# Load order, a copy in two halves, and a new instruction order in a four-layer transformer kernel

## The chip, the cores and the metric

The kernel runs on one core of a Trainium2 chip. A core has five engines that run side by side, each with its own in-order list of instructions: TensorE (PE, matrix products into PSUM), VectorE (DVE), ScalarE (ACT), GpSimd (POOL) and SyncE (SP, which here only issues DMA transfers). They wait for each other through semaphores. PSUM has eight banks of 512 columns. The metric is the time of one execution on the device in microseconds, as the median of several runs; smaller is better.

## What is computed

Two layers of linear attention (A) and two of a dense network with ReLU (B) alternate over a residual stream of 2048 tokens and 512 features:

```python
def _layernorm(x, axis=-1, eps=1e-5):
    m = jnp.mean(x, axis=axis, keepdims=True)
    v = jnp.var(x, axis=axis, keepdims=True)
    return (x - m) / jnp.sqrt(v + eps)
...
def _A_ref(x, wqkv, wo):          # 32 heads of 16
    ...
    phi = lambda t: jnp.where(t > 0, t + 1, jnp.exp(t)) + 1e-6
    pq, pk = phi(q), phi(k)
    kv = jnp.einsum("bhsd,bhse->bhde", pk, v)
    z = jnp.einsum("bhsd->bhd", pk)
    num = jnp.einsum("bhqd,bhde->bhqe", pq, kv)
    den = jnp.einsum("bhqd,bhd->bhq", pq, z)[..., None] + 1e-6
    o = num / den
    return (lambda x, *d: x.transpose(*d))(o, 0, 2, 1, 3).reshape(B, S, D) @ wo
def _B_ref(x, w1, w2):            # 1376 hidden features
    h = jnp.einsum("bsd,df->bsf", x, w1)
    h = jnp.maximum(h, zero)
    return jnp.einsum("bsf,fd->bsd", h, w2)
...
x = x + _A_ref(_layernorm(x, axis=-1), A_wqkv, A_wo)
x = x + _B_ref(_layernorm(x, axis=-1), B_w1, B_w2)
x = x + _A_ref(_layernorm(x, axis=-1), A_wqkv, A_wo)
x = x + _B_ref(_layernorm(x, axis=-1), B_w1, B_w2)
```

## The kernel before

**Tiles and chunks.** The 2048 tokens are 16 tiles of 128 (tile *i*), in four chunks of four. Tiles 0, 1, 2 and 3 are chunk 0; tiles 4 to 7 are chunk 1. Layers are numbered 0 to 3, and a step's full name has the layer ahead of it (`0.kproj2`).

**Loads.** All inputs stay in SBUF once loaded. `ld_x(lo, hi)` brings token tiles lo to hi-1 in one DMA, `ld_w` a slice of the attention weights. In this text they go by their keys: x0, x1 (one tile each), x2 (tiles 2 and 3), x4 (tiles 4 to 7), x8 and x12 (four tiles each); wka and wkb, the first and second half (by rows) of the K weights; wqa and wqb, the same of the Q weights; wv0, the V weights; wvl, one row of them broadcast to all partitions; wo, w1, w2a and w2b. wka is issued from ACT's queue, all other loads from SP's. SP issues in its own list's order, and each issue occupies it for about half a microsecond.

**The start of layer 0**, for each tile *i* (`ln_first`, L1668): `bnst` and `bnag` on DVE give mean and variance (L847, L848); `lnv` and `rstd` on ACT (or `veps` on DVE and `rstd` on POOL) the reciprocal root; `fnorm` on DVE the normed tile `xn` (L885). Tiles 0 to 5 are then transposed on PE: `trp` makes four 128x128 transposes into one PSUM bank, and `trev` copies the bank to `Tb`, on ACT for tiles 0 to 3 (`transpose_pe`, L905). Tiles 6 and 7 and all later ones are transposed by DMA, two tiles at a time: `tr1_1` is that of tiles 6 and 7, `tr2_0` and `tr2_1` those of chunk 2 (L898). `fill0` is eight products of zeros that keep PE running between `trp0` and `trp1` (L838).

Then come the projections. `kproj`*i* multiplies a tile by the K weights (four products of 512 columns, accumulated in a bank); for tiles 0 and 1 it is split by the weights' halves, `kproj0_0` (wka) and `kproj0_1` (wkb), so that the first can run before wkb is there (L973). The Q projection of chunk 0 runs in sixteen pieces `qh0_`*h_j_k*: tiles *2h* and *2h+1*, output block *j*, weight half *k* (wqa or wqb; L1196). Every K or Q bank is read by ACT twice, `_lin` (plus one) and `_exp`, and the larger is taken on DVE (`_em`, `_phi`), which gives phi. `wvless0` to `wvless3` on DVE subtract wvl from the V weights (L1110).

**Between layers 0 and 1.** `g` products sum phi(k) against the normed tiles; `gev` copies them out (L1141); `kv` and `kvmask` make the block-diagonal products, `m` multiplies them by wo, and `mev` copies the result `Mf` (L1166). `den` products give the denominators, `lnd` and `rdc` on ACT their reciprocals, and sixteen DMAs `spread`*t_j* broadcast these across partitions (L1223). `pqs` on DVE scales phi(q) (L1230), `fin`*i*`_0` and `fin`*i*`_2` are the halves of the output product of tile *i*, `resid` on DVE adds it to the stream, `sq` on ACT gives the squares for the next norm. From layer 1 on, products of 2x2 blocks are formed with seven multiplications instead of eight, and the sums that this needs are spread over ACT and DVE (names with `hv`, `hc`, `hs`, `p1` to `p7`, `c11` to `c22`).

**What sets the order.** The source creates operations in a fixed sequence, and each gets an index. A table `HINTS` (L63 on, about 1900 entries) adds a number to each, and each engine executes its operations strictly in order of the sum:

```python
op.prio = op.idx + HINTS.get(op.key, 0)      # L422
WINDOW = {PE: 1, ACT: 1, DVE: 1, POOL: 1, SP: 1}
```

An entry with "!" chooses the engine where there are two (0 or 1, an index into the operation's alternatives; for `trev`, `gev` and `mev` 0 is ACT and 1 is DVE). A planner (`_list_schedule`, L464) goes through these lists with assumed durations, hands out the PSUM banks, and so finds which waits have to be written. `LOAD_LATE` (L53) holds its assumptions on how late each load lands. Neither the assumed times nor the assumed lateness reach the chip; order, engines, banks and waits do.

Of the kernel before, what the change touches and what calls it, by code (L numbers as in the profile page):

```python
# [52 lines left out]
LOAD_LATE = {"x1": 320.0, "x2": 490.0, "wka": 780.0, "wkb": 540.0, "wqa": 1000.0, "x4": 1300.0, "wqb": 1260.0, "x12": 1060.0, "x8": 960.0, "wv0": 350.0}  # L53
# [9 lines left out]
HINTS = {"0.aqsum1": -43, "0.aqsum1!": 0, "0.aqsum2": -24, "0.aqsum2!": 0, "0.aqsum3": -126, "0.aqsum3!": 0, "0.aqsum4": 36,  # L63
# [302 lines left out]


class _Op:
# [1606 lines left out]
```

## Time and profile before

| | |
|---|---|
| runs | 262.16 us median of 3 (262.15 to 262.83) |
| the profiled execution, its own time | 262.21 us |
| its span, first to last instruction | 260.5 us |
| granted clock of TensorE | 1.000 of full speed |
| ACT, DVE, POOL: share of the span | 80%, 89%, 23% |
| DMA queue q1 (SP's): share of 16 engines' span | 35.8% |

In the views, PE is the matrix product, PEld the load of its weights, SPq the issue of a DMA. A row of the timeline reads: start and duration in us, engine, source line, operation, tile written <- tiles read, shape, how many are merged; in brackets, where there is one, the engine's idle time ahead of it and what ended it. A row of the chain in order of time reads: start, duration, what. A row of the DMA view ends with KB and us from issue to landing. A row of the windows reads: the stretch and its length, then the busy time of PE, PEld, DVE, ACT, POOL with the number of instructions, the granted clock, the DMA share and GB/s. A row of the waits reads: who <- for whom, us in total, times, longest. Most products have one source line (L953), so they are told apart by tiles and order.

### The profile page before, as it was taken

The page shows a single profiled execution, that of the slowest core. Times are in us where ns is not written, and L with a number is a line of the kernel's source. Part 1 is how long each engine was busy: PE and PEld are TensorE (multiplying, and loading weights), DVE is VectorE, ACT ScalarE, POOL GpSimd, SP SyncE. Part 2 cuts the span into 40 slices and gives each one's busy share as a digit, 9 for nine tenths or more (in the row PEclk, how much of TensorE's full clock was granted, in tenths as well). Part 3 has the DMA queues.
Part 4 walks back from the last instruction along what each step waited for, and adds up shares of the span by engine and source line. Part 5 has one row for each costly group of instructions (what it writes and reads, how often), then busy time and mean ns, then how long its engine had stood idle before and what let it go on. Part 6 is the DMA issues. An engine that isn't in the chain of part 4 may idle for free.

```text
span 260.5 us, 5888 instructions
## 1 busy us (share of the span) xinstructions
PE 255.3 (98%) x2176; PEld 198.9 (76%) x2176; DVE 230.7 (89%) x574; ACT 207.5 (80%) x446; POOL 60.0 (23%) x160
## 2 busy tenths in 40 slices
PE   7999999999999999999999999999999999999995
PEld 3555577834778898889888878774488988988884
DVE  4999998799989999999999899759999997876874
ACT  4999999579989988998899799786999946882200
POOL 4110000028745007240330340002875000000000
PEclk9999999999999999999999999999999999999999
DMA  7767951744351430434031030057442514200104
GB/s 206 277 148 140 330 189 21 183 101 97 68 67 32 87 58 12 91 42 63 0 60 25 0 73 11 3 113 172 95 80 50 82 23 128 56 20 3 81 3 161
DMA packets 45980, 22.46 MB, mean 86 GB/s; under 512 B 35872, under 2 KB 44416, under 8 KB 45952
## 3 DMA queue, kind: packets, MB, share of 16 engines
q1 hardware_dynamic: 45680, 21.83, 35.8%
q8 instruction: 17, 0.28, 0.4%
q10 hardware_dynamic: 272, 0.26, 0.4%
q14 instruction: 11, 0.09, 0.1%
HBM read 7.14 MB, written 2.10 MB: 35 GB/s over the span
## 4 chain that ended last, share of the span: by engine, by line
PE 85%; ACT 5%; DVE 4%; DMA 4%; SPq 1%; issue 1%
PE ps L953 84%; DVE xres L960 2%; DMA Tb<-xn 2%; SPq L1227 1%; ACT sqscr L968 1%; DMA big<-rdc 1%; DMA xin<-in_A_x_dram 1%; ACT xn L895 1%; DVE bst L847 1%; PE ps L914 0%; ACT rdc L1217 0%; DVE big L1235 0%; ACT escr L935 0%; ACT ps L700 0%; ACT lnd L1215 0%
## 5 line engine op out<-in xcount | busy, mean ns | idle before, releaser
L953 PE MATMUL ps<-w,big 128*128 128x256 bf16 (+1 forms) x256 | 32.3, 273 | 0.0
L968 ACT ACTIVATE sqscr<-xres 128x512 bf16<-128x512 f32 x48 | 29.8, 622 | 3.2 <-DVE xres L1623 1.6
L953 PE MATMUL ps<-big,xn 128*128 128x256 bf16 (+1 forms) x224 | 32.1, 288 | 0.0
L700 ACT ACTIVATE ps<-ps 128x512 f32<-128x512 f32 (+1 forms) x41 | 23.1, 573 | 10.5 <-PE ps L953 10.2
L953 PE MATMUL ps<-Mf,big 128*128 128x512 bf16 x128 | 28.6, 380 | 0.0
L953 PEld LDWEIGHTS ps<-w,big 128*128 128x128 bf16 (+1 forms) x256 | 25.0, 98 | 3.1
L953 PEld LDWEIGHTS ps<-big,xn 128*128 128x128 f16 x224 | 21.4, 98 | 6.3 <-issue 1.1
L953 PE MATMUL ps<-Tb,w 128*128 128x256 f16 x160 | 24.3, 273 | 0.0
L1436 DVE TENSOR_TENSOR big<-ps,escr 128x512 bf16<-128x512 f32 (+1 forms) x38 | 22.7, 601 | 1.3 <-ACT escr L1455 0.6
L953 PEld LDWEIGHTS ps<-Mf,big 128*128 128x128 bf16 x128 | 12.2, 98 | 14.5 <-ACT Mf L1166 0.5
L953 PE MATMUL ps<-xn,w 128*128 128x256 f16 x160 | 23.0, 273 | 0.0
L953 PE MATMUL ps<-xn,xin 128*128 128x256 f16 x160 | 22.7, 273 | 0.0
L953 PE MATMUL ps<-wqkv,Tb 128*128 128x512 bf16 (+1 forms) x96 | 20.3, 344 | 0.2 <-ACT Tb L920 0.2
L895 ACT ACTIVATE xn<-xres,nbias,rstd 128x512 f16<-128x512 f32 x24 | 19.1, 813 | 1.4 <-POOL nbias L879 1.4
L1455 ACT ACTIVATE escr<-ps 128x512 f32<-128x512 f32 (+1 forms) x38 | 18.7, 535 | 1.8 <-PE ps L953 1.8
L877 POOL TENSOR_TENSOR rstd<-veps,nhalf 128x2 f32<-128x2 f32 x24 | 18.2, 759 | 7.0 <-DVE veps L875 5.5
L869 POOL TENSOR_SCALAR mean<-s 128x2 f32<-128x2 f32 x24 | 7.2, 301 | 54.4 <-DVE xres L960 52.8
L1424 ACT ACTIVATE big<-ps 128x512 bf16<-128x512 f32 (+1 forms) x38 | 18.9, 527 | 0.4 <-PE ps L953 0.3
L953 PE MATMUL ps<-w,Tb 128*128 128x96 bf16 (+2 forms) x176 | 17.3, 225 | 0.6 <-DMA Tb<-xn 0.6
L953 PEld LDWEIGHTS ps<-Tb,w 128*128 128x128 bf16 x160 | 15.5, 98 | 2.3 <-DVE w L1384 0.2
L1445 ACT ACTIVATE big<-big 128x1024 bf16<-128x1024 bf16 (+1 forms) x16 | 14.3, 904 | 3.5 <-DVE big L1436 3.3
L953 PEld LDWEIGHTS ps<-xn,w 128*128 128x128 bf16 x160 | 15.5, 98 | 1.9 <-DVE xn L1402 0.2
(146 smaller groups left out, 639.6 us busy)
## 6 DMA issues: line engine op xcount, KB each, us to landing
big<-rdc SPq DMA_DIRECT2D x32, 128.0 KB, 2.7
xin<-in_A_x_dram SPq DMA_DIRECT2D x3, 512.0 KB, 7.0
w<-in_B_w_dram SPq DMA_DIRECT2D x1, 1376.0 KB, 7.0
w<-in_B_w_dram SPq DMA_DIRECT2D x1, 1280.0 KB, 10.1
wqkv<-in_A_wqkv_dram SPq DMA_DIRECT2D x3, 256.0 KB, 4.6
wqkv<-in_A_wqkv_dram SPq DMA_DIRECT2D x1, 512.0 KB, 4.5
wo<-in_A_wo_dram SPq DMA_DIRECT2D x1, 512.0 KB, 4.2
out_dram<-GT SPq DMA_DIRECT2D x1, 512.0 KB, 2.6
```

The costliest lines, as they stand in the source:

```text
L700: g.add(ACT, lambda e: e.activation(psv[:, b, 0:w], psv[:, src, 0:w], ACTF.Identity), [("ps", src)], [("ps", b)], C_ACT_PSUM if w == 512 e ...
L847: g.add(DVE, lambda e: e.bn_stats(bst[:, i, :], xin[:, i, :]), [("xin", i)] + list(after), [("bst", i)], C_DVE_BNST, name="bnst%d" % i)
L869: g.add(POOL, lambda e: e.tensor_scalar(mean[:, sl], s1[:, sl], -INV_D, None, ALU.mult), [("s1", i) for i in tl], [("mean", i) for i in tl ...
L877: g.add(POOL, lambda e: e.tensor_tensor(rstd[:, sl], veps[:, sl], nhalf[:, 0:n], ALU.pow), [("veps", lo), ("nhalf",)], [("rstd", i) for i ...
L895: (ACT, lambda e: e.activation(xn[:, i, :], src, ACTF.Identity, scale=rstd[:, i:i + 1], bias=nbias[:, i:i + 1]), C_ACT_SB_AP)],
L953: last = e.matmul(o, l, r, start=st, stop=sp, skip_group_check=skip)
L960: g.add(DVE, lambda e: e.scalar_tensor_tensor(xres[:, i, :], psv[:, b, :], 0.0, src, ALU.add, ALU.add, accum_out=s1[:, i:i + 1]), [("ps", ...
L968: g.add(ACT, lambda e: e.activation(sqscr[:, q, :], xres[:, i, :], ACTF.Square, scale=math.sqrt(INV_D), accum_out=s2[:, i:i + 1]), xr(i), ...
L1424: g.add_flex([(ACT, lambda e: e.activation(ap, src(), ACTF.Relu), C_ACT_PSUM if w == 512 else 270.0), (DVE, lambda e: e.tensor_scalar(ap, ...
L1436: g.add(DVE, lambda e: e.tensor_tensor(ap, sh(psv[:, bank, 0:w]), sh(other()), ALU.add), [("ps", bank)] + okeys + ([] if first else bk), q ...
L1445: g.add_flex([(ACT, lambda e: e.activation(row, row, ACTF.Relu), 945.0 if len(cs) == 2 else C_ACT_SB), (DVE, lambda e: e.tensor_scalar(row ...
L1455: g.add(ACT, lambda e, w=w: e.activation(q[:, 0:w], psv[:, bank, 0:w], ACTF.Identity), [("ps", bank)], key, C_ACT_PSUM if len(cs) == 2 els ...
```

## The change

Four things change.

The load of x2 goes ahead of that of wkb in SP's list, so x0, x1, x2, wkb, wqa, x4 instead of x0, x1, wkb, x2, wqa, x4. The planner's assumed lateness of x2, wka and wkb is raised by 100, 300 and 100 ns.

The transpose of tile 0 is split: `trp0_0` and `trp0_1` make two 128x128 transposes each into a bank of its own, and `trev0_0` and `trev0_1` copy 256 columns each. `kproj0_0` reads the first half of the tile alone. For this the tile's key in the dependence graph becomes two.

`trev2` and `trev3` may now run on DVE as well; by the new table `trev2` does.

`HINTS` is new in nearly all of its entries: of those that name a place, the median entry changes by 2 to 4 in each layer, the largest by 88, and 43 engine choices are the other way round. Among these, `gev0_2` and `mev0` go from DVE to ACT; `ld_wvl` goes from ahead of `tr2_1` and `tr2_0` to behind them in SP's list, `ld_w2b` from behind the first four spreads to behind all sixteen; the spreads of layer 0 come chunk 0, 2, 1, 3, with chunk 2's four ahead of chunk 1's (before, these eight were mixed); in ACT's list `lnv2`, `rstd2`, `lnv3`, `rstd3` come ahead of `k0_exp` (before, behind it).

```diff
-LOAD_LATE = {"x1": 320.0, "x2": 490.0, "wka": 780.0, "wkb": 540.0, "wqa": 1000.0, "x4": 1300.0, "wqb": 1260.0, "x12": 1060.0, "x8": 960.0, "wv0": 350.0}
+LOAD_LATE = {"x1": 320.0, "x2": 590.0, "wka": 1080.0, "wkb": 640.0, "wqa": 1000.0, "x4": 1300.0, "wqb": 1260.0, "x12": 1060.0, "x8": 960.0, "wv0": 350.0}
...
     def add(self, eng, emit, reads=(), writes=(), dur=100.0, lat=0.0, dma=False, name=""):
         if eng == ACT and name != "table" and not dma:
             reads = list(reads) + [("lnw",)]
+        reads, writes = ([x for k in ks for x in ([k + (0,), k + (1,)] if k[0] == "T" and len(k) == 2 else [k])] for ks in (reads, writes))
...
+        SPLIT_TREV = 1
...
         ld_w(slice(D, 2 * D), "wka", slice(0, 2), ACT)
         g.ops[-1].sdeps.append(g.last_w[("ident",)])
+        ld_x(2, 4)
         ld_w(slice(D, 2 * D), "wkb", slice(2, 4))
-        ld_x(2, 4)
...
         def transpose_pe(i):
-            b = alloc_bank(0)
...
+            parts = ((0, 1), (2, 3)) if i < SPLIT_TREV else ((0, 1, 2, 3),)
+            banks = [alloc_bank(0) for _ in parts]
+            for k, (b, cs) in enumerate(zip(banks, parts)):
...
+                    for q, c in enumerate(cs):
+                        last = e.transpose(psb()[:, 128 * q:128 * q + 128], xn[:, i, 128 * c:128 * c + 128], ident[:])
...
+                alts = [(ACT, lambda e, dst=dst, psb=psb, w=w: e.activation(dst, psb()[:, 0:w], ACTF.Identity), C_ACT_PSUM if w == 512 else 350.0),
+                        (DVE, lambda e, dst=dst, psb=psb, w=w: e.tensor_copy(dst, psb()[:, 0:w]), 345.0 if w == 512 else 240.0)]
+                g.add_flex(alts, [("ps", b)], [("T", i, c) for c in (range(2) if len(parts) == 1 else (k,))], name="trev%d%s" % (i, n))
             if i < 1:
                 warm_fill(i)
...
-            g.add_flex(alts[:1] if i < 4 else alts, [("ps", b)], [("T", i)], name="trev%d" % i)
...
                 mm_group(lambda cs=cs: [(psv[:, b, :], Tb[:, i, c, :], wqkv[:, c, D:2 * D], c == 0, c == 3, False) for c in cs],
-                         [("T", i)] + [(c,) for c in p if not isinstance(c, int)], [("ps", b)], len(cs) * C_MM512,
+                         [("T", i, h) for h in sorted({c // 2 for c in cs})] + [(c,) for c in p if not isinstance(c, int)], [("ps", b)], len(cs) * C_MM512,
```

More of the change, by code (lines that the diff above doesn't have):

```diff
@@ L60 @@
 WINDOW = {PE: 1, ACT: 1, DVE: 1, POOL: 1, SP: 1}
-HINTS = {"0.aqsum1": -43, "0.aqsum1!": 0, "0.aqsum2": -24, "0.aqsum2!": 0, "0.aqsum3": -126, "0.aqsum3!": 0, "0.aqsum4": 36,
[302 rows of a table removed]
+HINTS = {"0.aqsum1": -44, "0.aqsum1!": 0, "0.aqsum2": -4, "0.aqsum2!": 0, "0.aqsum3": -122, "0.aqsum3!": 0, "0.aqsum4": 2,
[302 rows of a table added]
 class _Op:
@@ L905, in transpose_pe, with psb, _emit @@
         def transpose_pe(i):
-            b = alloc_bank(0)
-            def psb():
-                return psv[:, b, 0:256].bitcast(F16)
-            def _emit(e, i=i):
-                last = None
-                for c in range(4):
-                    last = e.transpose(psb()[:, 128 * c:128 * c + 128], xn[:, i, 128 * c:128 * c + 128], ident[:])
-                return last
-            g.add(PE, _emit, [("xn", i), ("ident",)], [("ps", b), ("fill", i)], 4 * C_MM128, name="trp%d" % i)
+            parts = ((0, 1), (2, 3)) if i < SPLIT_TREV else ((0, 1, 2, 3),)
+            banks = [alloc_bank(0) for _ in parts]
+            for k, (b, cs) in enumerate(zip(banks, parts)):
+                def psb(b=b):
+                    return psv[:, b, 0:256].bitcast(F16)
+                def _emit(e, i=i, cs=cs, psb=psb):
+                    last = None
+                    for q, c in enumerate(cs):
+                        last = e.transpose(psb()[:, 128 * q:128 * q + 128], xn[:, i, 128 * c:128 * c + 128], ident[:])
+                    return last
+                n = "" if len(parts) == 1 else "_%d" % k
+                g.add(PE, _emit, [("xn", i), ("ident",)], [("ps", b), ("fill", i)], len(cs) * C_MM128, name="trp%d%s" % (i, n))
+                dst = Tb[:, i, cs[0]:cs[-1] + 1, :].rearrange("p c t -> p (c t)")
+                w = 128 * len(cs)
+                alts = [(ACT, lambda e, dst=dst, psb=psb, w=w: e.activation(dst, psb()[:, 0:w], ACTF.Identity), C_ACT_PSUM if w == 512 else 350.0),
+                        (DVE, lambda e, dst=dst, psb=psb, w=w: e.tensor_copy(dst, psb()[:, 0:w]), 345.0 if w == 512 else 240.0)]
+                g.add_flex(alts, [("ps", b)], [("T", i, c) for c in (range(2) if len(parts) == 1 else (k,))], name="trev%d%s" % (i, n))
             if i < 1:
                 warm_fill(i)
-            dst = Tb[:, i, :, :].rearrange("p c t -> p (c t)")
-            alts = [(ACT, lambda e: e.activation(dst, psb()[:, :], ACTF.Identity), C_ACT_PSUM),
-                    (DVE, lambda e: e.tensor_copy(dst, psb()[:, :]), 345.0)]
-            g.add_flex(alts[:1] if i < 4 else alts, [("ps", b)], [("T", i)], name="trev%d" % i)
         def esc_slots(n):
```

602 rows, old and new, of the table HINTS are left out of this document.

## The prediction

> **What bounds the kernel now.** I read the page's busy times first, then the chain of waits in order of time, then TensorE's waits, and last the timeline of the first 18 us.
>
> ```profile
> span 260.5 us, 5888 instructions
> ...
> PE 255.3 (98%) x2176; PEld 198.9 (76%) x2176; DVE 230.7 (89%) x574; ACT 207.5 (80%) x446; POOL 60.0 (23%) x160
> ```
> ```profile
> 70.18 4.40 DMA Tb<-xn
> ...
> 74.71 183.07 PE ps L953 x1674
> ```
> ```profile
> PE ps L953 <- DMA Tb<-xn: 0.6, 1, 0.6
> ```
>
> PE is the bound: 98% busy, and from 74.71 to 257.8, 183.07 us, the chain is one unbroken run of it. The change leaves the matrix work alone (the fillers and all transposes stay), so the time can move only by what PE stands idle. By PE's waits that is little: the one long wait after the warm-up, 0.6 us for a transposed tile, ends at 74.71. That reading is too kind: ends of matmuls are modelled and overlap the next start. The timeline's starts show more:
>
> ```profile
> 5.87 0.39 PE L914 MATMUL ps<-ident,xn 128*128 128x128 f16 x4
> 6.28 1.47 PE L953 MATMUL ps<-wqkv,Tb 128*128 128x512 bf16 x6
> ...
> 8.23 0.38 PE L953 MATMUL ps<-Tb,wqkv 128*128 128x256 f16 x2
> 8.78 0.72 PE L914 MATMUL ps<-ident,xn 128*128 128x128 f16 x8 [0.16 <-DVE xn L885]
> 9.34 0.38 PE L953 MATMUL ps<-Tb,wqkv 128*128 128x256 f16 x2
> 9.91 1.04 PE L953 MATMUL ps<-wqkv,Tb 128*128 128x512 bf16 x4 [0.19 <-ACT Tb L920]
> ...
> 73.70 0.38 PE L953 MATMUL ps<-xn,w 128*128 128x256 f16 x2
> ```
>
> Four 512-column products take 1.04 us, six 1.47, so one occupies PE for (1.47-1.04)/2 = 0.22 us, a 256-column one for 0.11, a 128-column transpose for 0.055. PE is therefore empty from 6.09 to 6.28 (0.19), from 8.45 to 8.78 (0.33) and from 9.56 to 9.91 (0.35): 0.9 us of holes ahead of kproj2 at 9.91. These the change can reach. At the wait above, PE is empty from 73.92 to 74.71, 0.8 us.
>
> **The change, part by part.** *Loads.* x2 and wkb swap places on SP.
>
> ```profile
> 1.71 0.43 SPq L768 DMA_DIRECT2D wqkv<-in_A_wqkv_dram  x1
> 2.18 0.47 SPq L763 DMA_DIRECT2D xin<-in_A_x_dram  x1
> ...
> 3.17 0.47 SPq L763 DMA_DIRECT2D xin<-in_A_x_dram  x1
> ```
> ```profile
> wqkv<-in_A_wqkv_dram SPq DMA_DIRECT2D x1, 256.0 KB, 4.0
> xin<-in_A_x_dram SPq DMA_DIRECT2D x1, 256.0 KB, 4.2
> ...
> xin<-in_A_x_dram SPq DMA_DIRECT2D x1, 512.0 KB, 6.0
> ```
>
> Issue plus time to landing: wkb now lands at 1.71 + 4.0 = 5.7, x2 at 2.18 + 4.2 = 6.4, x4 at 3.17 + 6.0 = 9.17. Both swapped loads are 256 KB, so they trade landings: x2 about 5.75 (bounds 5.3 and 6.4), wkb about 6.4 (5.75 and 6.8). Everything behind them, x4 first, has the same bytes ahead and stays.
>
> *The first copy in halves.* kproj0_0 needs only trev0_0.
>
> ```profile
> 5.63 1.27 ACT L920 ACTIVATE Tb<-ps 128x512 f16<-128x512 f16 x2 [0.50 <-PE ps L914]
> 7.35 0.60 ACT L935 ACTIVATE escr<-ps 128x512 bf16<-128x512 f32 x1 [0.46 <-PE ps L953]
> ```
> ```profile
> L1424 ACT ACTIVATE big<-ps 128x256 bf16<-128x256 f32 x14 | 5.4, 387 | 0.3 <-PE ps L953 0.3
> ```
>
> The copy starts at 5.63, after four transposes; two fewer bring it to about 5.45. A 256-wide copy takes 0.39 us (a whole one about 0.6), so the half is there near 5.84. But fill0 and trp1 still stand ahead of kproj0_0 on PE, until 5.87 + 4 x 0.055 = 6.09. So kproj0_0 moves from 6.28 to 6.09: 0.19, not 0.4. kproj0_1 follows at 6.53, just behind wkb; what wkb is later than that PE waits here. The price is 2 x 0.39 - 0.6 = 0.2 us of ACT, inside its 0.46 us of idleness ahead of 7.35.
>
> *Tiles 2 and 3.* Their statistics start at x2's landing: 5.77 instead of 6.42.
>
> ```profile
> 6.42 1.28 DVE L847 BATCH_NORM_STATS2 bst<-xin 128x6 f32<-128x512 bf16 x2 [0.85 <-DMA xin<-in_A_x_dram]
> ...
> 8.31 0.73 DVE L885 TENSOR_SCALAR xn<-xin,mv,rstd 128x512 f16<-128x512 bf16 x2 [0.39 <-ACT rstd L855]
> 9.18 1.29 DVE L847 BATCH_NORM_STATS2 bst<-xin 128x6 f32<-128x512 bf16 x2
> ...
> 17.00 0.42 DVE L921 COPY Tb<-ps 128x512 f16<-128x512 f16 x1
> ```
>
> The norms move from 8.31 to about 7.5 and 7.9. With trev2 on DVE (0.42, between 8.3 and 9.18, where DVE now norms) instead of behind two evacuations on ACT, kproj2 starts near 9.2, with one more pair of q products done ahead of it: a lead of 0.7 + 0.2 = 0.9 us. The two rsqrt pairs now stand ahead of k0_exp, which starts near 7.9 instead of 7.35; without trev2 (0.48) ACT is even again by k1_lin.
>
> *Where the lead goes.* Chunk 1's inputs come with x4 at 9.17. DVE takes them up at 9.18, at once, and from bnst7 to fnorm7 its new order is the old one.
>
> ```profile
> 12.39 1.35 SPq L900 DMA_TRANSPOSE Tb<-xn  x1
> ...
> 13.96 0.62 ACT L920 ACTIVATE Tb<-ps 128x512 f16<-128x512 f16 x1
> ...
> 14.71 2.03 PE L953 MATMUL ps<-wqkv,Tb 128*128 128x512 bf16 x8
> ...
> 15.69 0.55 PEld L953 LDWEIGHTS ps<-wqkv,Tb 128*128 128x128 f16 x4 [0.45 <-DMA Tb<-xn]
> ```
>
> So tr1_1 is still issued at 12.39, tiles 6 and 7 are transposed when they are now, and kproj7, the second half of the eight products from 14.71, starts at 15.70 as now. By the diff's hints (priority = index + hint) PE's list ahead of kproj7 holds the same products as before: trp0 to trp4, kproj0 to kproj4, all sixteen q halves. A PE that is 0.9 us early waits 0.9 us there, or already at kproj4, whose tile ACT finishes at 13.96 + 0.62 = 14.58 (six 512-wide evacuations stand between lnv6 and trev4 in both orders). Gain at 15.70: 0, bounds 0 and, were chunk 1 that much earlier, -0.9. Nothing points there; I take 0.
>
> *15.70 to 44.*
>
> ```profile
> 20.00:30.00 10.00, 10.00 (x58) 5.48 (x57) 10.00 (x31) 10.00 (x24) 0.56 (x2) 1.00 0.81 193
> ```
> ```profile
> 18.16 5.84 SPq L900 DMA_TRANSPOSE Tb<-xn  x3
> ...
> 23.97 1.09 DVE L1110 TENSOR_TENSOR wqkv<-wqkv,wvl 128x512 bf16<-128x512 bf16 x3
> ```
>
> PE, DVE and ACT are full here and keep their work, so a new order gains nothing. One step can lose: wvl's load goes behind the two transposes that SP issues from 18.16, to about 20.8. The loads above took 4.0 to 6.0 us to land, so 24.8 to 26.8. Its first use on DVE, 23.97 now, comes behind two wide maxima and some sums in the new order, near 25.8. I take 0 (nearest: the 256 KB loads) and keep +1.0, the wait at the late end.
>
> *44 to 75.* gev0_2 and mev0 leave DVE for ACT; w2b's issue moves behind the sixteen rdc spreads, of which chunk 1's now come last of the first twelve.
>
> ```profile
> 47.47 0.63 ACT L1217 ACTIVATE rdc<-lnd 128x512 bf16<-128x512 f32 x1
> ...
> 54.29 12.26 PE L953 MATMUL ps<-Mf,big 128*128 128x512 bf16 x56
> ...
> 55.10 0.68 DVE L960 SCALAR_TENSOR_TENSOR xres<-ps,xin 128x512 f32<-128x512 f32 x1
> ```
> ```profile
> 51.80 2.67 DMA big<-rdc
> ```
>
> rdc1 gets two more evacuations ahead of it (47.47 becomes 48.4 to 48.9) and ends 0.6 later; four issues of 0.6 then put the last landing at 53.5 to 54.0, not 51.80 + 2.67 = 54.47. resid1 then follows not pqs1_0, at 55.10, but fin1_2, which PE ends near 54.29 + 0.22 + 0.38 = 54.9. The chain to the transpose at 70.18 starts 0 to 0.2 earlier: I take 0.1. PE's list ahead of the wait at 74.71 again holds the same products, so that wait shrinks by this.
>
> *75 to the end.* No hole to close; changed places can only open one. I take 0.
>
> The sum against the profiled execution (262.21 us, span 260.5): 262.21 + 0 + 0 - 0.1 = 262.1. The median is 262.16, so execution and median are one.
>
> **A rule and a row.** The transpose that ends the wait at 74.71 took 4.40 us; the line's least and median are 3.0 and 3.2:
>
> ```profile
> DMA to landing us min/median/max: 3.0/3.2/4.8
> ```
> ```profile
> q8 instruction: 17, 0.28, 0.4%
> ```
> ```profile
> q8 instruction: 1, 0.02, 5.1%
> ```
>
> The last row is of the DMA queues from 71.9 to 73.2 us: one instruction packet, 5.1% of 16 engines' 1.3 us, so 1.06 us of one engine, inside the transpose's time. The Trainium skill, "Runtime: NRT & Kernel Launch", section "Instruction fetch mechanics", says that instructions come in blocks of 256 and that crossing a block is mostly hidden. The page's counts agree with the first (2176 products and 2176 weight loads are 17 x 256, the queue's count); the row speaks against the second, by which this wait would lack a cause and the next kernel would not have it.
>
> **The rivals.** *The wait at 74.71 goes (faster).* The transpose misses the instruction packet and lands up to 4.4 - 3.0 = 1.4 us earlier; PE's hole there, 0.8, is what counts: 262.1 - 0.8 = 261.3. For it: many small moves shift the two against each other. Against: the packet comes mid-burst, its number goes with PE's list, and PE's place and the issue both move under 0.2. Chance 0.22.
>
> *Another transpose meets one (slower).* The price is 1.4 us less the tile's cover; it decides where a tile is ready less than 1.4 ahead of PE. Between 75 and 257 no such wait shows, and the hints of all four layers change. With 0.4 of cover: 262.1 + 1.0 = 263.1. Against: the old order passes 183 us without one. Chance 0.2.
>
> *x2 doesn't land earlier.* It shares the engines with wka from ACT's queue. The lead shrinks, and since chunk 1 takes it anyway the time is 262.2: inside the forecast's own range, chance 0.08. The Trainium skill, "DMA: Bandwidth & Descriptors", section "Queues, rings and completion order", has each engine alternate between queues packet by packet; no row here shows that pair.
>
> **How the numbers follow.** Forecast 262.1, chance 0.5 (own range 261.6 to 262.6); faster 0.22; slower 0.2; x2 unchanged 0.08. The range, 261.2 to 263.1, reaches both ends, wvl's +1.0 among them. A measurement of this kernel can tell about 0.3% from no change, 0.8 us: under 261.4 is faster, over 262.9 slower. So: faster 0.22, same 0.58, slower 0.2.
>
> **What would show it.** Right: kproj0_0 near 6.1 and kproj2 near 9.2, yet PE empty for 0.7 to 1.0 us before kproj4 or kproj7, and kproj7 at 15.7; the long transpose and its wait still near 74.6. Wrong: kproj7 before 15.3 (chunk 1 was not the pace), a DVE wait near 25.8, PE idle anywhere after 75.

## The result, and the profile after

The changed kernel takes 264.06 us (median of 4 runs, 263.73 to 264.22), the kernel before 262.36 beside it; the ratio is 1.0063, with a 95% interval of 1.0044 to 1.0082. It is slower by 1.7 us. The forecast was 262.1 with a range to 263.1, so the time lies outside it, on the side to which 0.2 was given.

The profiled execution took 264.22 us, its span 262.3 beside 260.5. These rows are the page's head and busy times, the end of the chain of waits (start, length, what) and TensorE's waits (sum, times, longest) of the changed kernel.

```profile
span 262.3 us, 5888 instructions
...
PE 255.4 (97%) x2176; PEld 198.9 (76%) x2176; DVE 231.9 (88%) x577; ACT 203.8 (78%) x441; POOL 61.7 (24%) x163
```
```profile
70.42 0.70 ACT xn L897
71.12 0.02 ACT escr L1460
71.14 5.15 DMA Tb<-xn
76.30 0.14 issue
76.43 183.11 PE ps L958 x1674
```
```profile
PE ps L958 <- DMA Tb<-xn: 1.6, 1, 1.6
...
PE ps L958 <- ACT Tb L923: 0.5, 1, 0.5
```

The work is the same (255.4 us of PE), and the unbroken tail is the same: 183.11 us beside 183.07. It starts at 76.43 instead of 74.71, 1.72 us later, which is the whole loss of this execution (its span is 1.8 longer). The transpose that ends the wait (tiles 6 and 7 in layer 1, "the long transpose" below) takes 5.15 us instead of 4.40, and is issued at 71.14 instead of 70.18.

The timeline tells where the other part of the 1.72 us is. First VectorE, then TensorE of the changed kernel:

```profile
9.91 1.29 DVE L849 BATCH_NORM_STATS2 bst<-xin 128x6 f32<-128x512 bf16 x2 [0.93 <-DMA xin<-in_A_x_dram]
```
```profile
14.29 0.38 PE L958 MATMUL ps<-Tb,wqkv 128*128 128x256 f16 x2
15.20 1.04 PE L958 MATMUL ps<-wqkv,Tb 128*128 128x512 bf16 x4 [0.52 <-ACT Tb L923]
16.07 0.38 PE L958 MATMUL ps<-Tb,wqkv 128*128 128x256 f16 x2
16.41 0.39 PE L958 MATMUL ps<-wqkv,Tb 128*128 128x512 bf16 x1
...
74.43 0.38 PE L958 MATMUL ps<-Tb,w 128*128 128x256 f16 x2
```

x4 lands at 9.88, not 9.17; DVE waits 0.93 us for it, and kproj7 starts at 16.41 instead of 15.70: 0.71 us. From there PE is not empty any longer than before until 74.43 + 2 x 0.11 = 74.65, where it waits 1.78 us, to 76.43, instead of 0.80: 0.98 us. The two make 1.69 of the 1.72.

So I began with two theories. **A**: the swapped loads delay x4, and x4 sets the pace. **B**: the new order brings instruction packets into the long transpose. The rivals: the late x4 is chance; the order itself costs time.

### The profile page after: what moved, and what is told of

Same layout as the page of the kernel before. It is cut to its first block, busy times and chain, and to the rows that moved or that the text cites. A ratio compares the mean times of both kernels' runs of the same rounds, so it can differ in the third digit from the quotient of the medians.

```text
span 262.3 us, 5888 instructions
## 1 busy us (share of the span) xinstructions
PE 255.4 (97%) x2176; PEld 198.9 (76%) x2176; DVE 231.9 (88%) x577; ACT 203.8 (78%) x441; POOL 61.7 (24%) x163
## 4 chain that ended last, share of the span: by engine, by line
PE 84%; ACT 5%; DMA 5%; DVE 3%; issue 1%; SPq 1%; POOL 1%; DVEq 0%
PE ps L958 84%; DMA xin<-in_A_x_dram 3%; DMA Tb<-xn 2%; ACT sqscr L973 2%; ACT xn L897 1%; DVE big L1240 1%; DVE xres L965 1%; ACT big L938 1%; DVE bst L849 0%; ACT ps L702 0%; ACT escr L940 0%; SPq L770 0%; POOL var L875 0%; SPq L765 0%; ACT escr L1460 0%
## 5 line engine op out<-in xcount | busy, mean ns | idle before, releaser
L1429 ACT ACTIVATE big<-ps 128x512 bf16<-128x512 f32 (+1 forms) x35 | 18.1, 548 | 7.2 <-PE ps L958 7.0
L958 PE MATMUL ps<-Tb,w 128*128 128x256 f16 x160 | 23.7, 273 | 0.0
L897 ACT ACTIVATE xn<-xres,nbias,rstd 128x512 f16<-128x512 f32 x26 | 20.6, 811 | 0.4 <-POOL nbias L881 0.2
L879 POOL TENSOR_TENSOR rstd<-veps,nhalf 128x2 f32<-128x2 f32 x24 | 18.8, 787 | 5.8 <-DVE veps L877 5.2
L958 PEld LDWEIGHTS ps<-xn,xin 128*128 128x128 bf16 x160 | 15.2, 98 | 1.8
```

The source lines that it names most:

```text
L879: g.add(POOL, lambda e: e.tensor_tensor(rstd[:, sl], veps[:, sl], nhalf[:, 0:n], ALU.pow), [("veps", lo), ("nhalf",)], [("rstd", i) for i ...
L897: (ACT, lambda e: e.activation(xn[:, i, :], src, ACTF.Identity, scale=rstd[:, i:i + 1], bias=nbias[:, i:i + 1]), C_ACT_SB_AP)],
L958: last = e.matmul(o, l, r, start=st, stop=sp, skip_group_check=skip)
L1429: g.add_flex([(ACT, lambda e: e.activation(ap, src(), ACTF.Relu), C_ACT_PSUM if w == 512 else 270.0), (DVE, lambda e: e.tensor_scalar(ap, ...
```

## The experiments

In all of them "the wait" is PE's empty time ahead of the long transpose's first reader, by starts of matmuls as in the prediction; "landing" is from issue to landing. The place and length of instruction packets are those of the trace's packet records: the 16 KB ones are TensorE's, as their count was 17 in the prediction; the 8 KB ones are on another queue (q14). Ratios are to the kernel before on the same chip. There is one trace for each kernel, while the executions of one kernel lie up to 3.8 us apart (e14_warm36, 262.44 to 266.23): the waits of a trace account for that execution and not for the median.

### Theory A: the loads

`e1_swap_only` is the kernel before with the load order alone, `e2_no_swap` the changed kernel with the old load order, `after_again` the changed kernel unaltered.

```diff
 # e1_swap_only, from the kernel before; e2_no_swap is the reverse on the changed kernel
+        ld_x(2, 4)
         ld_w(slice(D, 2 * D), "wkb", slice(2, 4))
-        ld_x(2, 4)
 # and the places of ld_x2 and ld_wkb in HINTS (4 and 7)
```

> The kernel before with nothing changed but the order of two loads (tiles 2 and 3 ahead of the second half of the K weights). Theory A (the swap pushes back every load behind it, and tiles 4 to 7 set the pace up to kproj7): x4 lands near 9.9 instead of 9.2, kproj7 begins 0.5 to 0.8 us later than 15.70, and the time is 0.5 to 0.8 us above the kernel before, 262.8 to 263.2. Rival (the swap is harmless and the new order of the instructions did it all, or the late x4 was chance): x4 within 0.2 of 9.2, time within 0.3 us of the kernel before.

> The changed kernel with the two loads put back into the old order; the order of instructions on TensorE, VectorE, ScalarE and GpSimd is the new one, and the first copy stays in halves. Theory A: x4 lands near 9.2, kproj7 begins at 15.5 to 15.8 instead of 16.41, and the time falls by 0.6 to 0.9 us, to about 263.3; what is left above the kernel before is the wait near 75. Rival (the new order did it all): 264.0 within 0.3.

> The changed kernel once more, unaltered. Theory A had tiles 4 to 7 land 0.7 us late through the swap (9.88); the swap alone gave 9.27, so if that delay was chance of one execution, x4 lands at 9.0 to 9.5 here and kproj7 begins at 15.8 to 16.1, while the time stays at 263.5 to 264.5 through the wait near 75, again 1.6 to 2.0 us. If the swap and the new order together delay it, x4 is at 9.7 to 10.0 again and kproj7 at 16.3 to 16.5.

Measured: the swap alone 262.16 us, ratio 0.9995 (0.9973 to 1.0016), x4 at 9.27. Without the swap the changed kernel stays slow: 264.59, ratio 1.0102 (1.0045 to 1.0160; four executions, 263.67 to 266.63), x4 at 9.41, wait 1.90. Unaltered a second time: 264.29, ratio 1.0081 (1.0052 to 1.0109), and in its profiled execution (263.25 us, the fastest of six) x4 lands at 9.26. VectorE and TensorE of that execution:

```profile
9.29 1.29 DVE L849 BATCH_NORM_STATS2 bst<-xin 128x6 f32<-128x512 bf16 x2 [0.56 <-DMA xin<-in_A_x_dram]
```
```profile
15.77 1.04 PE L958 MATMUL ps<-wqkv,Tb 128*128 128x512 bf16 x4
...
66.95 1.05 PE L958 MATMUL ps<-Tb,w 128*128 128x256 f16 x8 [0.33 <-DVE w L1389]
...
75.46 0.84 PE L958 MATMUL ps<-w,Tb 128*128 128x96 bf16 x16 [0.88 <-DMA Tb<-xn]
```

Theory A falls: kproj7 is at 15.77 here, and the median is as high as in the first runs. In this execution the tail starts at 75.46, 0.75 later than in the kernel before; the wait is 1.04, not the 1.6 to 2.0 expected. (The hole ahead of 66.95 costs nothing by itself: the tail starts when the transpose has landed.) The late x4 is no rule: over all 20 traces of this study x4 lands at 8.59 to 9.42 in 18, and late in two, at 9.88 in the first profile and at 9.81 in e16_pool_order (below). Both have the swapped loads, as eleven of the 20 have; whether the swap makes a late x4 more frequent stays open, but e1_swap_only and e10_new_to42 (below), which have the swap and the old order behind 42 us, cost nothing.

### Theory B: move the instruction packets

The packets' places should hang on how many instructions an engine has behind it (they do: 24 more products in e7_warm128 moved the packet at 71.98 to 68.56). So I changed these numbers without changing the work: 16 filler products for 8 (`e4_fill16` on the kernel before, `e4a_fill16` on the changed one), 2 fillers of 512 columns for 8 of 128 (`e5_fill512`), the 8 warming products of 512 columns as 32 of 128 (`e7_warm128`, `e7a_warm128`), and one clearing of a tile on GpSimd as 16 pieces (`e6_pool16`).

```diff
-                for k in range(WARM):
-                    last = e.matmul(psv[:, wt, :], wrm[:, 0:128], wrm[:, :], start=True, stop=True)
+                for k in range(4 * WARM):   # e7_warm128, e7a_warm128
+                    last = e.matmul(psv[:, wt, 0:128], wrm[:, 0:128], wrm[:, 0:128], start=True, stop=True)
...
-                for k in range(8):
+                for k in range(16):         # e4_fill16, e4a_fill16
...
-        g.add(POOL, lambda e: e.memset(hr[:], 0.0), ...
+        g.add(POOL, lambda e: [e.memset(hr[:, k // 8, k // 2 % 4, 64 * (k % 2):64 * (k % 2) + 64], 0.0) for k in range(16)][-1], ...   # e6_pool16
```

> The kernel before with 16 filler products of 128 columns where 8 were: 0.45 us more of work at full clock in a stretch that waits for tiles 4 to 7 anyway, and every later instruction of TensorE lies 8 products further back in the code. Theory B (the late transpose of tiles 6 and 7 in layer 1 is held by an instruction packet whose place in time is set by where the code stands): the landing of that transpose, 4.40 us after its issue before, changes by at least 0.3 us either way, and the wait of 0.8 at 74.7 with it; the time moves by as much. Rival (the length of that transpose is its own or is set by the transposes of that moment): 4.2 to 4.6 us, time within 0.3 us of the kernel before.

> The changed kernel with 16 filler products where 8 were. Theory B: the landing of the transpose of tiles 6 and 7 in layer 1 (5.15 us after its issue, with two instruction packets in it) changes by at least 0.3 us, and the wait of 1.78 at 76.4 with it; if the second packet then misses it, the time falls by about 0.8 us to 263.2. Rival: 5.0 to 5.3 us again and 264.0 within 0.3, or above it by the 0.45 us of the fillers if the stretch does not cover them.

> The kernel before with its 8 filler products of 128 columns written as 2 of 512: the same columns, 12 instructions of TensorE fewer ahead of everything later, so its 16 KB packets come some 1.3 us later. Theory B: the one at 71.98 moves to about 73.3 and so out of the transpose of tiles 6 and 7 in layer 1, which lands 3.0 to 3.4 us after its issue; the wait of 0.8 at 74.7 goes and the time falls by 0.6 to 0.9 us, to about 261.6, unless another transpose that TensorE waits for is met. Rival: landing 4.2 to 4.6 us, no change.

> The changed kernel with one clearing of a tile on GpSimd, in a stretch where that engine is idle (2.4 to 9.5 us), written as 16 small ones: the same work, 15 more instructions of GpSimd ahead of everything later. Theory B for the second packet (the 8 KB instruction packet of 1184 ns at 74.71 is GpSimd's, and it falls into the long transpose because of where GpSimd's code stands): it comes some 8 us earlier, the transpose of tiles 6 and 7 in layer 1 lands 0.4 to 0.9 us sooner after its issue than 5.15, and the time falls by as much, to 263.2 to 263.7. Rival (the packet is VectorE's or ScalarE's, or the length of the transpose does not hang on it): the 8 KB packet is still within 0.3 us of the same place beside the transpose, landing 5.0 to 5.3 us after the issue, time 264.0 within 0.3.

> The kernel before with the 8 warming products of 512 columns at its start written as 32 of 128 columns: the same columns, 24 more products, so that every later instruction of TensorE lies 48 instructions (with weight loads) further back. Theory B: the 16 KB packets of TensorE come 4 to 6 us earlier, none at 72; the transpose of tiles 6 and 7 in layer 1 lands 3.0 to 3.4 us after its issue instead of 4.4, the wait of 0.8 at 74.7 goes, and the time falls by 0.6 to 0.9 us, to about 261.4, if no other transpose that TensorE waits for is met. Rival (the long transpose has another cause): 4.2 to 4.6 us, time within 0.3 of the kernel before.

> The changed kernel with the warming products written as 32 of 128 columns. Theory B: the 16 KB packet leaves the transpose of tiles 6 and 7 in layer 1; only the 8 KB one may still meet its end: it lands 3.0 to 4.1 us after its issue instead of 5.15, the wait near 76 falls from 1.78 to between 0 and 0.8, and the time falls by 1.0 to 1.8 us, to 262.2 to 263.0. Rival (the change's new order itself costs the time there): landing 5.0 to 5.3, time 264.0 within 0.3.

| kernel | us, ratio (interval) | TensorE's packet: start after the issue, length | landing | wait |
|---|---|---|---|---|
| before | 262.4 | 1.80, 1.06 | 4.40 | 0.80 |
| e4_fill16 | 265.17, 1.0124 (1.0079 to 1.0169) | 1.06, 1.06 | 4.02 | 0.59 |
| e5_fill512 | 263.90, 1.0057 (1.0039 to 1.0075) | 1.02, 1.37 | 4.29 | 0.82 |
| e7_warm128 | 263.99, 1.0053 (1.0035 to 1.0072) | none | 3.03 | none |
| after | 264.06, 1.0063 (1.0044 to 1.0082) | 1.02, 1.29 | 5.15 | 1.78 |
| after_again | 264.29, 1.0081 (1.0052 to 1.0109) | 0.24, 1.07 | 4.42 | 1.04 |
| e4a_fill16 | 264.81, 1.0117 (1.0072 to 1.0163) | 0.09, 1.01 | 4.02 | 0.64 |
| e6_pool16 | 263.88, 1.0051 (1.0033 to 1.0068) | 1.25, 1.56 | 5.54 | 2.17 |
| e7a_warm128 | 263.07, 1.0028 (1.0010 to 1.0047) | none | 3.94 | 0.57 |

The mechanism is seen best in the row of bytes moved. These are GB/s in 40 slices of 0.225 us, from 69 to 78 us: of the kernel before, of the changed kernel, and of e14_warm36 (told below), in which no packet comes near.

```profile
GB/s 217 204 201 156 7 0 0 0 0 0 75 224 209 283 197 166 16 1 8 10 9 76 0 0 0 0 0 0 0 0 0 0 0 0 0 0 132 222 213 212
```
```profile
GB/s 0 0 132 221 215 208 201 175 14 0 0 0 0 0 97 197 205 132 17 2 9 9 9 214 272 127 8 7 7 0 0 0 0 0 0 0 0 0 0 0
```
```profile
GB/s 212 205 77 157 287 121 0 0 0 0 0 34 212 220 206 215 197 82 0 0 36 0 0 0 0 0 0 0 0 0 0 0 0 0 155 220 217 204 197 163
```

The third row is a transpose alone: five slices near 200 between two partial ones and it is done (3.05 us with its issue; the 36 behind it is an 8 KB packet). In the first, most of the bytes are through and the rest trickles at 1 to 16 GB/s for five slices, which fits one engine of sixteen that works off its share behind the packet. In the second the packet comes in the middle: the second half doesn't start for five slices (17 2 9 9 9), and behind it there is a tail (8 7 7). Two 8 KB packets lie near this tail, 0.35 us at 74.33 and 1.18 us at 74.71.

What follows. Theory B holds for the long transpose: with no packet of TensorE in it the wait goes in e7_warm128, and it shrinks from 1.78 to 0.57 in e7a_warm128. But misses stand beside it. e4_fill16 and e4a_fill16 brought the packet into the transpose of tiles 6 and 7 of layer 0 (5.05 and 4.91 us instead of 3.2, and TensorE waited 1.7 and 1.5 us for it). e7_warm128 lost at 63.7, 109.9 and 200.0 (0.40, 1.0 and 0.71 us) what it had won. In e5_fill512 the packet came no later at all but earlier, at 71.35. Its place varies between executions even of the same code: 1.02 and 0.24 us behind the issue in the two of the changed kernel. And e6_pool16 moved the 8 KB packet of GpSimd from 74.7 to 66.5, as predicted, without shortening the transpose: the tail stayed, with the other 8 KB packet (0.36 us) still beside it, and the time, 263.88, is hardly below the changed kernel's.

### Where in the order the time is lost

`e8_late_old` takes the new order up to 20 us of planned time and the old one behind it, `e9_late_new` the reverse; `e10_new_to42` and `e11_new_from42` are cut at 42 us, the end of the projections.

```diff
 # e10_new_to42, its table written as a rule: each entry of HINTS by the operation's planned start in the kernel before
-HINTS = new
+HINTS = {k: (new if planned[k] < 42000.0 else old)[k] for k in names}
```

> Half the change by time: up to 20 us the changed kernel (loads swapped, first copy in halves, new order), from there on the old order on every engine, instruction for instruction. Theory C (the time is lost in the new order behind 20 us: the transpose of tiles 6 and 7 in layer 1 is issued later after kproj7 than before and is held longer by instruction packets): it is issued 54.4 to 54.6 us after kproj7 begins, lands 4.2 to 4.7 us later, the wait is 0.6 to 1.1 us, and the time is within 0.4 us of the kernel before. Rival (the loss lies in the first 20 us: the loads or the halves): 1.0 to 1.8 us above the kernel before.

> The other half: up to 20 us the kernel before, from there on the new order on every engine, instruction for instruction. Theory C: the transpose of tiles 6 and 7 in layer 1 is issued 54.7 to 55.3 us after kproj7 begins, lands 4.4 to 5.5 us after its issue, the wait near 76 is 1.0 to 2.0 us, and the time is 1.0 to 1.8 us above the kernel before. Rival (first 20 us): within 0.4 us of the kernel before.

> The first half of the change again, cut at the end of the projections (42 us) instead of 20 us, because the cut at 20 us left ScalarE waiting 0.66 for VectorE's statistics at the joint: the changed kernel up to 42 us, the old order from there on. Theory C (the loss is made behind 42 us): no idle time of TensorE between 17 and 52 us beyond that of the kernel before, the transpose of tiles 6 and 7 in layer 1 issued 54.4 to 54.7 us after kproj7 begins and landed 4.0 to 4.7 us later, and a time within 0.5 us of the kernel before. Rival (the first 42 us hold a good part of the loss): 0.8 us or more above the kernel before, with the idle time up to kproj7 or before 42 us.

> The other half: the kernel before up to 42 us, the new order on every engine behind it. Theory C: that transpose issued 54.7 to 55.3 us after kproj7 begins, a 16 KB packet of TensorE starting 0.2 to 1.4 us after the issue instead of 1.8, landing 4.4 to 5.7 us after the issue, the wait near 76 of 1.0 to 2.3 us, and the time 1.0 to 2.0 us above the kernel before. Rival: within 0.5 us of the kernel before.

The cut at 20 us was a bad one: e8_late_old took 264.51, ratio 1.0084 (1.0057 to 1.0111), but lost 1.4 us at 25 to 27 us, at the joint. ScalarE's row there:

```profile
20.57 0.21 ACT L855 ACTIVATE veps<-mv 128x4 f32<-128x4 f32 x1 [0.66 <-DVE mv L850]
```

Its wait for the long transpose was 0.87, that of the kernel before. e9_late_new took 264.48, ratio 1.0089 (1.0056 to 1.0122), with a wait of 2.29 (in its profiled execution TensorE's products also took twice as long from 78 to 81.5 us, at a granted clock of 0.51). The cut at 42 us is clean: **the first 42 us, with the swap, the halves and the new order, cost nothing**: 262.63, ratio 0.9998 (0.9981 to 1.0014), wait 0.99. The rest alone costs: 263.65, ratio 1.0039 (1.0020 to 1.0059), landing 4.73, wait 1.37. That is less than the whole change's 1.0063 and 1.0081; the intervals touch, and I can't say whether the parts add up. In the trace of e11_new_from42 the tail starts 0.91 later than in the kernel before, and TensorE loses another 0.68 at 156.85, where it waits for a later transpose.

### What takes the loss away

`e13_both_moved` is the changed kernel with the edits of e7a_warm128 and e6_pool16 together.

> The changed kernel with both shifts of the code at once: warming products as 32 of 128 columns and the cleared tile of GpSimd in 16 pieces. With the first alone the time was 263.07 and the transpose of tiles 6 and 7 in layer 1 was still held to 3.94 us by an 8 KB packet of 689 ns at 2.86 us after its issue. Theory B: with that packet gone too it lands 3.0 to 3.3 us after its issue, TensorE does not wait for it (less than 0.2 us near 76), and the time is 262.3 to 262.9, that of the kernel before: the loss of the change was the meeting with the packets. Rival (the new order costs time by itself): 263.0 or more with a landing of 3.0 to 3.3 us.

262.58 us, ratio 1.0014 (0.9991 to 1.0037): no loss is left that these runs can show, though the wait was 0.45, not under 0.2. Its wait row, behind 20 us:

```profile
PE ps L958 <- DMA Tb<-xn: 0.3, 1, 0.3
```

The transpose landed in 3.82 with no TensorE packet in it, not in the 3.0 to 3.3 expected. Its bytes, from 69 to 78 us:

```profile
GB/s 184 218 207 209 224 115 2 0 0 0 0 0 73 223 209 205 243 186 46 7 8 2 0 0 0 0 0 0 0 0 0 0 0 0 0 41 217 217 209 212
```

There is a tail again (7 8 2), and an 8 KB packet ahead of it, not the one that was moved: 0.31 us, 2.09 behind the issue, in the slice of 243. The six long transposes without a packet of TensorE divide by it: with an 8 KB packet that starts 2.09 to 2.21 us behind the issue they took 3.82 to 3.94 (e7a_warm128, e13_both_moved, e17_all_three), with one at 2.63 or later 3.03 to 3.05 (e7_warm128, e14_warm36, e15_warm40). Another transpose of 1056 packets, near 111 us, shows the same in all traces: 3.07 and 3.08 where no packet starts in its first 3 us (e10_new_to42, e9_late_new), 3.75 to 3.97 in the seventeen with one 8 KB packet at 1.78 to 2.62, and 4.71 in e5_fill512, where a packet of TensorE comes on top. So a small packet holds a transpose as well, by some 0.7 to 0.9 us. No run moved this one away.

The shift of TensorE's code that helped here cost the kernel before 1.4 us (e7_warm128), so a time alone can't tell a cure from a lucky draw. The traces show no luck behind the long transpose: neither after, after_again nor e13_both_moved has a hole there, so what differs between these three stands ahead of it.

Comparing the traces I then found what issues it later. VectorE and GpSimd of the kernel before, then of the changed one, where VectorE subtracts 128x2 numbers (the variance of tiles 4 and 5) while GpSimd norms tile 3:

```profile
61.95 0.73 DVE L1235 TENSOR_TENSOR big<-big 128x1024 bf16<-128x1024 bf16 x1
62.61 0.15 DVE L873 TENSOR_TENSOR var<-s,nm 128x2 f32<-128x2 f32 x1
62.68 0.68 DVE L960 SCALAR_TENSOR_TENSOR xres<-ps,xin 128x512 f32<-128x512 f32 x1
```
```profile
61.79 0.20 POOL L871 TENSOR_TENSOR nm<-mean 128x2 f32<-128x2 f32 x1
61.97 1.27 POOL L890 TENSOR_SCALAR xn<-xres,mean,rstd 128x512 f16<-128x512 f32 x1
```
```profile
62.49 0.71 DVE L1240 TENSOR_TENSOR big<-big 128x1024 bf16<-128x1024 bf16 x1
63.12 0.56 DVE L875 TENSOR_TENSOR var<-s,nm 128x2 f32<-128x2 f32 x1
63.61 0.68 DVE L965 SCALAR_TENSOR_TENSOR xres<-ps,xin 128x512 f32<-128x512 f32 x1
```
```profile
62.08 0.19 POOL L873 TENSOR_TENSOR nm<-mean 128x2 f32<-128x2 f32 x1
62.23 0.19 POOL L881 TENSOR_TENSOR nbias<-mean,rstd 128x2 f32<-128x2 f32 x1
62.41 1.27 POOL L892 TENSOR_SCALAR xn<-xres,mean,rstd 128x512 f16<-128x512 f32 x1
```

0.56 us instead of 0.15, and it ends at 63.68, with GpSimd's norm (62.41 + 1.27). The next residuals, and with them the chain to the long transpose, start 0.4 us later. Over 18 traces (all but the two told next) this divides the orders without exception: 0.15 in the nine with the old order behind 42 us, 0.56 to 0.65 in the nine with the new one, each time ending within 8 ns of the norm. `e16_pool_order` puts four small operations of GpSimd ahead of that norm back; `e17_all_three` does so in e13_both_moved.

```diff
-         "0.nmean4": 3, "0.msq4": 7, "0.rstd2#2": 28
+         "0.nmean4": 7, "0.msq4": 9, "0.rstd2#2": 27
```

> The changed kernel with four small operations of GpSimd near 61 us (rstd, mean, nbias and the squared mean ahead of the norm of tile 3) back in the old order, nothing else. In the nine executions with the old order behind 42 us VectorE's variance of tiles 4 and 5 took 0.15 us, in the nine with the new one 0.56 to 0.65, always ending with GpSimd's norm. Theory D (the place of that norm against VectorE's small operation makes the chain to the transpose of tiles 6 and 7 some 0.45 us later): the variance takes 0.15 again, the transpose is issued 0.3 to 0.5 us earlier after the transpose of layer 0 has landed than the 55.1 of the changed kernel, and the time falls by 0.2 to 0.5 us to 263.6 to 263.9. Rival (these four have no part in it): 0.56 to 0.65 again, time within 0.2 us of the changed kernel's 264.1.

> The same four operations in the kernel whose packets of TensorE and GpSimd were moved (262.58 and a wait of 0.45 at 74.6). Theory D: the transpose is issued 0.3 to 0.5 us earlier, the wait of 0.45 falls under 0.15, and the time is 262.1 to 262.4, at or just below the kernel before. Rival: 262.4 to 262.8 with the wait of 0.3 to 0.6 again.

The variance takes 0.15 in both. From the landing of layer 0's transpose of tiles 6 and 7 to the issue of the long one it is 54.55 us in e16_pool_order and 54.35 in e17_all_three, where the nine with the new order had 55.10 on average (54.78 to 55.40). That measure is a poor one: the nine with the old order have 54.53 to 56.24 by it, since other waits lie in the stretch. From the start of the first residual to the issue the split is clean: 15.02 to 15.08 us in the eleven traces whose variance took 0.15 (these two among them), 15.50 to 15.57 in the other nine. The variance costs the chain 0.42 to 0.55 us, and putting back the four operations on GpSimd takes this away. e16_pool_order: 263.75, ratio 1.0052 (1.0032 to 1.0072), below the changed kernel's 1.0063 and 1.0081, but the intervals overlap: its long transpose still meets the packets (landing 5.72, wait 2.22). e17_all_three: **262.07 us, ratio 0.9989 (0.9969 to 1.0010)**. Its timeline, against the kernel before's at 74.71:

```profile
73.67 0.38 PE L958 MATMUL ps<-Tb,w 128*128 128x256 f16 x2
74.04 0.84 PE L958 MATMUL ps<-w,Tb 128*128 128x96 bf16 x16
```

PE waits 0.16 us there, and the tail starts 0.67 earlier than in the kernel before. It is the fastest version of this study by its median; that it beats the kernel before is not shown, nor that it beats e13_both_moved, whose interval overlaps its own.

With this the start of the tail can be followed in each trace: it is the sum of three columns and 0.13 to 0.14 us.

| execution | first residual | from there to the issue | landing | tail starts |
|---|---|---|---|---|
| before | 55.10 | 15.08 | 4.40 | 74.71 |
| after | 55.64 | 15.50 | 5.15 | 76.43 |
| after_again | 55.35 | 15.55 | 4.42 | 75.46 |
| e13_both_moved | 55.13 | 15.51 | 3.82 | 74.59 |
| e16_pool_order | 55.79 | 15.05 | 5.72 | 76.69 |
| e17_all_three | 54.98 | 15.06 | 3.86 | 74.04 |

The 1.72 us of the first profile are 0.54 of a later first residual, in the execution with the late x4, 0.42 of the variance and 0.75 of a longer transpose. e13_both_moved still pays the variance; it is level because its transpose is 0.58 shorter than that of the kernel before.

### A shift alone is no cure

`e14_warm36` and `e15_warm40` are the kernel before with still more, smaller warming products (28 of 128 and 8 of 64 columns; 24 and 16).

> The kernel before with the warming products as 28 of 128 and 8 of 64 columns: the same columns, 56 instructions of TensorE more ahead of everything later, where the run with 48 more had no wait at 74.7 but met its packets at 92.7 and further on. Theory B: the transpose of tiles 6 and 7 in layer 1 lands 3.0 to 3.4 us after its issue and the wait there is under 0.1; if no later transpose that TensorE waits for is met, the time is 261.5 to 261.9, below the kernel before; for each one met 0.5 to 1.0 us come on top. Rival (the landing hangs on something else): 4.2 to 4.7 us and the time of the kernel before.

> The same with 24 products of 128 and 16 of 64 columns, 64 instructions of TensorE more. Theory B: as with 56, the packet near 68 some 0.9 us earlier again, so that it may meet the transpose issued at 67.5 or 68.4 (landing over 3.5 us instead of 3.0); in layer 1 no wait for tiles 6 and 7, time 261.5 to 261.9, and 0.5 to 1.0 us more for each transpose that is met and waited for. Rival: as above.

Both took the wait at 74.7 away: the long transpose lands in 3.05 us, as the third row of GB/s above shows. Both kernels are slower nevertheless: 264.60, ratio 1.0075 (1.0042 to 1.0108), and 265.01, 1.0092 (1.0060 to 1.0124). TensorE of e14_warm36 near 198 us:

```profile
197.07 0.82 PE L953 MATMUL ps<-Tb,w 128*128 128x256 f16 x6
198.48 1.03 PE L953 MATMUL ps<-xn,xin 128*128 128x256 f16 x8 [0.59 <-ACT big L1424]
```

It is empty for 0.76 us here, in a stretch where the kernel before never was; in e15_warm40 for 1.32 at 200.1, and for 0.40 to 0.76 at three other places. That explains only part: e14_warm36's profiled execution took 262.61, its median is 264.60.

## Why the prediction was wrong

**The step that failed** is the last of the sum but one: "The chain to the transpose at 70.18 starts 0 to 0.2 earlier: I take 0.1", and with it "so that wait shrinks by this". Its parts: rdc1 near 48.4 to 48.9 was right (48.60 in e11_new_from42), but the last landing that it leads to was not at 53.5 to 54.0: SP issued chunk 1's four at 49.36, 50.00, 51.27 and 51.92, since one of them took 1.23 us and not 0.6, and the last landed at 54.55, 0.08 later than before. These rows are the chain of e11_new_from42:

```profile
51.92 2.63 DMA big<-rdc
...
62.71 0.57 DVE var L873
...
70.75 4.74 DMA Tb<-xn
```

The first residual came 0.08 later, at 55.18 instead of 55.10, and the chain lost another 0.4 at the variance, 0.57 on the chain instead of 0.15. So it started 0.57 later (70.75), not 0.1 earlier. I had compared the lists of operations, and no list shows this: the same operation in the same place on VectorE costs four times as much because GpSimd's norm stands a little differently.

**The price of the wait** failed with it. I had weighed only that the long transpose might lose its packet (261.3) or that another one might meet one (263.1). That this same transpose could be held longer, 5.15 us instead of 4.40 and up to 5.72 in these runs, was no case of mine. Yet it is the nearest: I had argued that "PE's place and the issue both move under 0.2", but in the two executions of the changed kernel the issue moved by 0.72 and 0.96; the packet's place moves by 0.8 us from one execution to the next, and a packet in the middle of the transfer holds its second half too. With the waits of 1.04 to 2.29 us, measured in the runs with the new order in which TensorE's packets were left alone, where I kept 0.7, the sum would have been 262.4 to 263.7.

What was right, by the steps:

- *Loads*: x2 at 5.51 (forecast 5.75, bounds 5.3 to 6.4), wkb at 6.57 (6.4). "Everything behind them, x4 first, has the same bytes ahead and stays": right in nine of the eleven traces with the swap, and wrong by 0.7 in the profiled one. The third rival, that x2 lands no earlier, fails: it landed at 5.51 to 5.99 in the eleven traces with the swap and at 6.13 to 7.20 in the nine without. Whether wka pays for it no trace settles (4.96 to 6.21 with the swap, 4.49 to 5.85 without).
- *Halves*: kproj0_0 at 6.41 and 6.00 (6.09). *Tiles 2 and 3*: norms at 7.56 (7.5); kproj2 at 9.73 and 9.16 (near 9.2).
- *The lead is lost*: as said, "already at kproj4", which starts at 15.20 after 0.69 empty. e10_new_to42 shows the whole of it: nothing gained or lost in 42 us.
- *wvl*: landed at 25.22 (24.8 to 26.8), and VectorE, at 26.56, doesn't wait for it. *75 to the end*: 183.11 beside 183.07.

**The rule that was weighed.** With no packet of TensorE in it the long transpose took 3.03 to 3.94 us (six traces, the upper three with an 8 KB packet), with one 4.02 to 5.72 (fourteen). The Trainium skill, "Runtime: NRT & Kernel Launch", section "Instruction fetch mechanics", calls the crossing of a block mostly hidden. For TensorE's own stream nothing here speaks against that; for a transfer that shares a DMA engine with the packet the runs do.

## What to carry to other kernels

When one wait is left and it ends with a DMA, look at what else its DMA engines carried: a small code packet can hold a whole transpose, and any edit ahead of it, of work or of code alone, draws that lot again. An order that removes holes ahead of a stretch which something else paces gains nothing, so price the next late tile before the hole. And when the order of GpSimd changes, compare the durations of VectorE's small operations, not only their places.

## What the runs showed of the hardware

- A 16 KB instruction packet of TensorE took 0.89 to 1.67 us on one DMA engine; a DMA transpose of 1056 packets that takes 3.03 to 3.05 us alone took 4.02 to 5.72 with it. An 8 KB packet of 0.31 to 0.57 us was enough to make it 3.75 to 3.97. The packet's place is not fixed by the code: 1.02 and 0.24 us behind the issue in two executions of one kernel.
- A subtraction of 128x2 numbers on VectorE took 0.15 us or 0.56 to 0.65, beside the same norm on GpSimd, which itself took 1.27 to 1.32 us here and 0.77 at its least in the kernel before. It passed when it started 0.57 to 0.64 us behind the norm's start (eleven traces) and was held to the norm's end when it started 0.68 to 0.72 behind (nine). In the eleven the norm had started 0.02 to 0.04 us behind VectorE's operation ahead of the variance, in the nine 0.08 ahead of it. The Trainium skill, "SBUF — State Buffer", section "SBUF: two separate sides", has VectorE and GpSimd share a pair of ports under an exclusive lock, which the one that starts first holds for a whole instruction; the nine, whose ends agree within 8 ns, look like that. The eleven don't, by the recorded starts: there the variance passed though the norm had started before it. Why is open.
- The same load landed up to 1.3 us apart between executions (x4 at 8.59 to 9.88). Single packets of its time took over 1 us in late executions and in punctual ones alike (1.31 us in the first of the changed kernel, 1.40 in the kernel before), so they don't tell why.
